# Induced attention and channel mix on one core: the large products as 64-row halves on two row tiles

## The chip, the cores and the metric

The kernel runs on one core of one Trainium2 chip. Five engines work side by side, each through its own queue in order: TensorE (PE in the profile, with its weight loads as PEld), VectorE (DVE), ScalarE (ACT), GpSimd (POOL) and SyncE (SP), whose queue issues nearly all DMAs. The metric is the device time of one execution in microseconds; each number of a run is the median of its executions.

## The reference

Two layers follow each other. The first is attention over 32 inducing points, the second a channel mix with a squared ReLU and a sigmoid gate. Cut to what matters:

```python
# x: (4, 12608, 128); inducing: (32, 128); w_k: (128, 1024); w_v: (1024, 128); w_r: (128, 128)
def mab(q, kv):
    s = scale * (q @ kv.transpose(0, 2, 1))
    a = np.exp(s - s.max(-1, keepdims=True))
    a /= a.sum(-1, keepdims=True) + 1e-09
    return a @ kv
h = mab(I, x)                       # (4, 32, 128)
x = mab(x, h)                       # (4, 12608, 128)
x_prev = np.concatenate([zeros, x[:, :-1, :]], axis=1)      # one token back
xk = mu_k * x + (1.0 - mu_k) * x_prev
xr = mu_r * x + (1.0 - mu_r) * x_prev
k = np.maximum(xk @ w_k, 0.0)
v = k * k @ w_v
r = 1.0 / (1.0 + np.exp(-(xr @ w_r)))
return r * v
```

## The kernel before

**Low rank.** The second attention is never multiplied out. A token's row of x is its 32 weights a times h, so xk @ w_k is a (32 numbers) times h·diag(mu_k)·w_k plus the weights of the token before times h·diag(1−mu_k)·w_k. The kernel makes these small matrices once per batch (tile `W`, in the function `combine`) and keeps for each group of 512 tokens the transposed weights (tile `R`).

**Precision.** Products use fp32r operands. To keep fp32 accuracy each operand is split into a rounded high part and the low rest. In the way up (`up`, lines 780 and 782) the four products high·high, high·low, low·high and low·low of 32 rows each are stacked into the 128 rows of one matmul: `R` holds high, low, high, low, `W` holds high, high, low, low. One such matmul takes the tokens, a second one the tokens shifted by one (a column of `R` ahead of the group, filled by `halo`). In the way down (`down`, line 811) three passes wvh·kh, wvl·kh and wvh·kl run over 128 rows each.

**Units.** A batch has 25 groups (24 of 512 tokens and one of 320). A group has four units, each with two of the eight 128-wide chunks of the 1024 hidden channels; the four batches make 400 units. A unit n issues, in the order that the main loop writes out by hand:

- on PE four matmuls up (128x512 each) into one of two buffers of `ps_a`; two more for the gate (`zgate`) once per group; then the six matmuls down of unit n−4 (`LAG`) into the group's bank `ps_v`;
- on DVE the ReLU (`k_t`, line 792) and, for some units (`high_vector`), the square kh (line 794); otherwise ACT makes kh (797); ACT makes the full square (798);
- on POOL the low part kl = k² − kh (line 800), which the way down reads four units later;
- after a group's last unit, on DVE, the product with the gate (`oT`, 816) and one unit later a transpose (`ot`, 827); every second group SP issues four stores (834).

**Work between the units.** Hand-written tables (`at`, `soon`) put the attention of the batch in hand (`stage_b`) and the first attention of the next batch (`stage_a`, `combine`) behind units. `stage_a` transposes x on DVE (331) and scatters it with four DMAs to `xt` (334), then makes scores (359) and the weighted sum (428) on PE. `stage_b` makes scores (617), softmax, the high and low parts `ah` and `al`, and spreads them with four DMAs per group (671) and one DMA for the halo column (594) into `R`; ten buffers of `R` let this run ahead. Nothing on PE waits for SP other than for a DMA that has landed.

**In the head** a short warm-up (`spin`, lines 895 to 902) runs three 128-row matmuls, four pairs of 64-row matmuls, and three 128-row matmuls again.

Of the kernel before, what the change touches and what calls it, by code (L numbers as in the profile page):

```python
# [8 lines left out]
F32 = mybir.dt.float32  # L9
# [6 lines left out]
EPS = 1e-9  # L16


@with_exitstack
def kernel(  # L20
# [22 lines left out]
    WF = F + C  # L43
# [4 lines left out]
    assert NBLK == 7 and C == P and M * Q == P and F % 1024 == 0 and TAIL % Q == 0  # L48
# [8 lines left out]
    r_pool = ctx.enter_context(tc.tile_pool(name="r_pool", bufs=10))  # L57
# [153 lines left out]
    def stage_a_head(j):  # L211
# [38 lines left out]
        def expo():  # L250
            L.e1t = mp.tile([P, G], F32, name="rT")
# [221 lines left out]
    def combine(b, at=None, t=0):  # L473
# [18 lines left out]
        def weights():  # L492
# [11 lines left out]
            sw = sm.tile([P, P], F32, name="mk", bufs=1)  # L504
            if ahead:
                nc.vector.tensor_scalar(out=sw, in0=stack_f, scalar1=wt, scalar2=rd,
                                        op0=ALU.mult, op1=ALU.mult)
            else:
                nc.vector.tensor_scalar(out=sw, in0=stack_f, scalar1=rd, scalar2=None, op0=ALU.mult)
            L["sw"] = sw  # L510

        def mixed(*parts):
            for nm, mu in parts:
                h4 = L["h4"][nm] = sm.tile([P, P], F32, name="h4" + nm, bufs=1)
                nc.vector.tensor_scalar(out=h4, in0=L["hp"], scalar1=mu, scalar2=None, op0=ALU.mult)

        def hfin():
            ps = pb_tile(None if ahead else "b")
            nc.tensor.matmul(out=ps[:, :P], lhsT=S.acc, rhs=L["sw"], start=True, stop=True)
            h = sm.tile([P, P], F32, name="hT")  # L520
            nc.vector.tensor_copy(out=h, in_=ps[:, :P])
            S.hT = h[:, :M]
            L["hp"] = ps[:, :P]
            L["h4"] = {}
            mixed(("k0", muk), ("k1", omuk))
            mixed(("r0", mur), ("r1", omur))
            S.W = [wp.tile([P, WF], F32R, name=f"W{s}") for s in range(2)]

        def wpart(s, c, tile):

            X = {}
            c0, cw, nm, src = ((F, C, f"r{s}", wr_sb) if c is None else
                               (c * G, G, f"k{s}", wk_sb[:, c * G:(c + 1) * G]))
            dst = S.W[s][:, c0:c0 + cw]

            def prod():
                X["ps"] = tile()[:, :cw]
                nc.tensor.matmul(out=X["ps"], lhsT=L["h4"][nm], rhs=src, start=True, stop=True)

            def high():  # L540
                nc.scalar.copy(out=dst, in_=X["ps"])

            def low():
                nc.vector.tensor_tensor(out=dst[P // 2:], in0=X["ps"][P // 2:, :],
                                        in1=dst.bitcast(F32)[P // 2:], op=ALU.subtract)
            return prod, high, low

        def wpack(parts, cw, tags, t):

            X = {}  # L550
            rows = M * len(parts)

            def prod():
                X["ps"] = pb_tile("a")
                for n, (s, nm, c0, src) in enumerate(parts):
                    nc.tensor.matmul(out=X["ps"][M * n:M * (n + 1), :cw], lhsT=L["h4"][nm][:, :M], rhs=src,
                                     start=True, stop=True)

            def high():
                X["hi"] = st.tile([P, G], F32R, name=tags[0], bufs=tags[2])[:rows, :cw]  # L560
                nc.scalar.copy(out=X["hi"], in_=X["ps"][:rows, :cw])

            def low():
                lo = st.tile([P, G], F32R, name=tags[1], bufs=tags[2])[:rows, :cw]
                hi = X["hi"].bitcast(F32)
                nc.vector.tensor_tensor(out=lo, in0=X["ps"][:rows, :cw], in1=hi, op=ALU.subtract)
                X["hl"] = (hi, lo.bitcast(F32))

            def spread(n):
                s, nm, c0, src = parts[n]  # L570
                for q in range(Q):
                    nc.sync.dma_start(out=S.W[s].bitcast(F32)[M * q:M * (q + 1), c0:c0 + cw],
                                      in_=X["hl"][q // 2][M * n:M * (n + 1)])
            at(t, prod)
            at(t, high)
            at(t + 1, low)
            for n in range(len(parts)):
                at(t + 1 + n, lambda n=n: spread(n))
# [5 lines left out]
        parts = [(s, f"k{s}", c * G, wk_sb[:, c * G:(c + 1) * G]) for c in range(F // G) for s in range(2)]  # L584
        for n in range(0, len(parts), Q):
            wpack(parts[n:n + Q], G, ("ah", "al", 1), t + 11 + 4 * (n // Q))
        wpack([(s, f"r{s}", F, wr_sb) for s in range(2)], C, ("xs", "xs", 3), t + 13)

    def halo(S, g, far=True):

        if g == 0:
            nc.vector.memset(S.R[g].bitcast(F32)[:, 0:1], 0.0)
        elif far:
            nc.sync.dma_start(out=S.R[g].bitcast(F32)[:, 0:1], in_=S.R[g - 1].bitcast(F32)[:, G:G + 1])
        else:
            nc.vector.tensor_copy(out=S.R[g][:, 0:1], in_=S.R[g - 1].bitcast(F32)[:, G:G + 1])


    def stage_b(b, j, at, t):
# [55 lines left out]
        def high():  # L655
            L["ah"] = st.tile([P, G], F32R, name="ah")[:, :w]
            nc.scalar.copy(out=L["ah"], in_=L["aT"])

        def low():
            L["al"] = st.tile([P, G], F32R, name="al")[:, :w]  # L660
            nc.vector.tensor_tensor(out=L["al"], in0=L["aT"], in1=L["ah"].bitcast(F32), op=ALU.subtract)

        def spread(i):
            src = (L["ah"].bitcast(F32), L["al"].bitcast(F32))
            if full or i == 0:
                S.R[j * Q + i] = r_pool.tile([P, G + 1], F32R, name="R")
                halo(S, j * Q + i)
            R = S.R[j * Q + (i if full else 0)].bitcast(F32)
            o, lo = (0, 0) if full else (offs[i], i * w - offs[i])
            for q in range(Q):  # L670
                nc.sync.dma_start(out=R[M * q:M * (q + 1), 1 + o + lo:1 + o + w],
                                  in_=src[q % 2][M * i:M * (i + 1), lo:w])
# [12 lines left out]
        for i in range(Q):  # L685
            at(t + 10 + i, lambda i=i: spread(i))

    def stage_b_head(gs):
# [7 lines left out]
        def scores():  # L696
            ps = L["ps"] = pb_tile("b")
            for k, g in enumerate(gs):
# [5 lines left out]
                S.R[g] = r_pool.tile([P, G + 1], F32R, name="R")  # L704
# [19 lines left out]
        def place(k):  # L724
            g = gs[k]
            X = {}

            def src():
                return L["s2"][:, k * Q:(k + 1) * Q, :].unsqueeze(2).broadcast_to([P, Q, 2, M])

            def high():
                X["a"] = st.tile([P, G], F32R, name=("ah", "al")[g % 2]) \
                    .rearrange("p (k q m) -> p k q m", k=Q, q=Q)
                nc.scalar.copy(out=X["a"][:, :, 0::2, :], in_=src())
# [220 lines left out]
    def start():  # L955
# [9 lines left out]
        def gate_bank(s):  # L965
            if s == 0:
                box["g"] = bank()
# [112 lines left out]
```

## Time and profile before

| | |
|---|---|
| time, median of 3 runs | 1143.82 us (1141.26 to 1147.39) |
| profiled execution | 1144.99 us, its span 1142.9 us, granted clock 0.993 |
| PE busy | 1103.4 us (97%) |
| PEld busy | 837.4 us (73%) |
| DVE busy | 917.7 us (80%) |
| ACT busy | 971.3 us (85%) |
| POOL busy | 948.4 us (83%) |
| chain that ended last, by engine | PE 79%, DVE 8%, ACT 7% |
| DMA moved | 102.32 MB, mean 90 GB/s |

Busy time of PE counts a matmul from its start to the end of its pipeline, so the mean of one (393 ns for 128x512) is longer than the distance to the next start. The share says how seldom PE stands still; the rate is read from the distance between starts. Issuing a DMA holds SP's queue but counts as no engine's busy time.

### The profile page before, as it was taken

To read this page: it belongs to the slowest core of one execution; us is meant where nothing else is said; L and a number is where in the kernel's file an instruction comes from. 1 tells how busy PE (TensorE), PEld (TensorE's weight loads), DVE (VectorE), ACT (ScalarE), POOL (GpSimd) and SP (SyncE) were. 2 spreads that over 40 slices of the span, in tenths; PEclk is the share of its full clock that TensorE was granted. 3 is DMA by queue.
4 is the path that set the end of the run, shared out by engine and by line. 5 is a ranking of instruction groups with operands and counts; after the bars stand their busy time and mean duration, and the time that the engine had idled before them with its cause. 6 is when DMAs were issued, how large, how long until landed. Compare 5 with 4: busy or idle time off the path is not lost.

```text
span 1142.9 us, 17673 instructions
## 1 busy us (share of the span) xinstructions
PE 1103.4 (97%) x5716; PEld 837.4 (73%) x5716; DVE 917.7 (80%) x1294; ACT 971.3 (85%) x1107; POOL 948.4 (83%) x413
## 2 busy tenths in 40 slices
PE   6778999999989999999999999999999999999997
PEld 4456777777777777777877777777778777777886
DVE  5687898987678889897777889898777888887665
ACT  5477889888988888888988988889889988889996
POOL 1157888998887988888889888888888899999996
PEclk9999999999999999999999999999999999999999
DMA  9213444555135455555124455545222233242212
GB/s 275 69 28 91 106 108 111 129 127 108 31 70 119 91 121 124 125 124 124 24 61 87 110 128 120 129 99 124 50 50 61 46 64 59 54 74 56 43 28 34
DMA packets 274988, 102.32 MB, mean 90 GB/s; under 512 B 234288, under 2 KB 249808, under 8 KB 272592
## 3 DMA queue, kind: packets, MB, share of 16 engines
q1 hardware_dynamic: 274560, 101.18, 40.7%
q8 instruction: 45, 0.74, 0.3%
q14 instruction: 47, 0.39, 0.1%
q10 hardware_dynamic: 336, 0.02, 0.0%
HBM read 28.07 MB, written 25.82 MB: 47 GB/s over the span
## 4 chain that ended last, share of the span: by engine, by line
PE 79%; DVE 8%; ACT 7%; issue 3%; SPq 2%; DMA 1%; DVEq 0%; ACTq 0%
PE ps_v L811 40%; PE ps_a L780 15%; PE ps_a L782 13%; DVE k_t L792 3%; PE pb_b L617 2%; PE ps_v L769 2%; PE ps_v L770 2%; PE pb_a L359 2%; ACT kh L797 2%; PE pb_a L428 2%; ACT L772 1%; ACT L634 1%; ACT k_t L798 1%; SPq L93 1%; DVE kh L794 1%
## 5 line engine op out<-in xcount | busy, mean ns | idle before, releaser
L800 POOL TENSOR_TENSOR kl<-k_t,kh 128x1024 fp32r<-128x1024 f32 (+2 forms) x400 | 939.6, 2377 | 154.1 <-ACT k_t L798 136.4
L792 DVE TENSOR_SCALAR k_t<-ps_a 128x1024 f32<-128x1024 f32 (+1 forms) x400 | 480.2, 1201 | 162.1 <-PE ps_a L782 147.0
L798 ACT ACTIVATE k_t<-k_t 128x1024 f32<-128x1024 f32 (+1 forms) x400 | 418.3, 1048 | 46.9 <-DVE kh L794 35.7
L797 ACT ACTIVATE kh<-k_t 128x1024 fp32r<-128x1024 f32 (+1 forms) x352 | 366.0, 1040 | 81.5 <-PE ps_v L811 45.0
L780 PE MATMUL ps_a<-R,W 128*128 128x512 f32 (+1 forms) x800 | 324.5, 406 | 8.9 <-DMA R<-al 4.8
L782 PE MATMUL ps_a<-R,W 128*128 128x512 f32 (+1 forms) x800 | 314.3, 393 | 0.0
L811 PE MATMUL ps_v<-kh,wvh 128*128 128x512 f32 (+1 forms) x800 | 249.8, 393 | 5.3 <-ACT rT L772 4.7
L811 PE MATMUL ps_v<-kh,wvl 128*128 128x512 f32 (+1 forms) x800 | 249.3, 393 | 0.0
L811 PE MATMUL ps_v<-kl,wvh 128*128 128x512 f32 (+1 forms) x800 | 249.1, 392 | 0.1
L780 PEld LDWEIGHTS ps_a<-R,W 128*128 128x128 f32 x800 | 151.4, 189 | 82.9 <-issue 19.9
L811 PEld LDWEIGHTS ps_v<-kh,wvh 128*128 128x128 f32 x800 | 149.4, 189 | 44.0 <-ACT rT L772 10.0
L811 PEld LDWEIGHTS ps_v<-kl,wvh 128*128 128x128 f32 x800 | 150.3, 189 | 34.8 <-POOL kl L800 0.4
L811 PEld LDWEIGHTS ps_v<-kh,wvl 128*128 128x128 f32 x800 | 150.4, 189 | 34.1
L782 PEld LDWEIGHTS ps_a<-R,W 128*128 128x128 f32 x800 | 151.3, 189 | 30.7
L816 DVE TENSOR_TENSOR oT<-ps_v,rT 128x512 f32<-128x512 f32 (+1 forms) x100 | 66.7, 667 | 2.3
L827 DVE STREAM_TRANSPOSE ot<-oT 128x512 f32<-128x512 f32 x96 | 67.2, 700 | 0.0
L794 DVE SCALAR_TENSOR_TENSOR kh<-ps_a,k_t 128x1024 fp32r<-128x1024 f32 x48 | 58.8, 1225 | 5.4 <-DVE k_t L792 0.5
L772 ACT ACTIVATE rT<-ps_v 128x512 f32<-128x512 f32 (+1 forms) x99 | 57.3, 579 | 0.3
L331 DVE STREAM_TRANSPOSE xs<-xb 128x512 f32<-128x512 f32 x72 | 50.0, 694 | 2.5 <-DMA xt<-xs 1.2
L772 ACT ACT_TABLE_LOAD x31 | 39.8, 1283 | 0.5
L769 PE MATMUL ps_v<-R,W 128*128 128x512 f32 (+1 forms) x99 | 39.2, 396 | 0.8 <-DVE oT L816 0.8
L770 PE MATMUL ps_v<-R,W 128*128 128x512 f32 (+1 forms) x99 | 38.9, 393 | 0.0
(196 smaller groups left out, 614.8 us busy)
## 6 DMA issues: line engine op xcount, KB each, us to landing
out_dram<-ot SPq DMA_DIRECT2D x184, 128.0 KB, 3.3
xb<-in_x_dram SPq DMA_DIRECT2D x18, 1024.0 KB, 5.6
xt<-xs SPq DMA_DIRECT2D x288, 64.0 KB, 2.0
R<-ah SPq DMA_DIRECT2D x184, 64.0 KB, 2.0
R<-al SPq DMA_DIRECT2D x184, 64.0 KB, 2.0
kh<-in_x_dram SPq DMA_DIRECT2D x4, 512.0 KB, 7.3
kl<-in_x_dram SPq DMA_DIRECT2D x4, 512.0 KB, 7.5
xb<-in_x_dram SPq DMA_DIRECT2D x8, 256.0 KB, 5.8
```

The lines of the kernel that those rows point to most:

```text
L769: nc.tensor.matmul(out=ps[:, :w], lhsT=S.W[0][:, F:WF], rhs=R[:, 1:w + 1], start=True, stop=False)
L772: nc.scalar.activation(out=self.rT, in_=ps[:, :w], func=AF.Sigmoid)
L780: nc.tensor.matmul(out=ps[:, c, :w], lhsT=S.W[0][:, cs], rhs=R[:, 1:w + 1], start=True, stop=False)
L782: nc.tensor.matmul(out=ps[:, c, :w], lhsT=S.W[1][:, cs], rhs=R[:, 0:w], start=False, stop=True)
L792: nc.vector.tensor_scalar(out=k, in0=self.ps[:, :, :w], scalar1=0.0, scalar2=None, op0=ALU.max)
L794: nc.vector.scalar_tensor_tensor(out=kh, in0=self.ps[:, :, :w], scalar=0.0, in1=k, op0=ALU.max, op1=ALU.mult)
L797: nc.scalar.activation(out=kh, in_=k, func=AF.Square)
L798: nc.scalar.activation(out=k, in_=k, func=AF.Square)
L800: return lambda eng, a, z: eng.tensor_tensor(out=kl[:, :, a:z], in0=k[:, :, a:z], in1=kh.bitcast(F32)[:, :, a:z], op=ALU.subtract)
L811: nc.tensor.matmul(out=self.v, lhsT=wt[:, fc, :], rhs=kk[:, c, :], start=(fc == 0 and n == 0), stop=(fc == FC - 1 and n == 2))
L816: nc.vector.tensor_tensor(out=self.oT, in0=self.v, in1=self.rT, op=ALU.mult)
L827: nc.vector.transpose(out=ot[:, o:o + w], in_=self.oT)
```

## The change

**Way up.** The 32-row parts are stacked anew. Rows 0 to 63 of `W` belong to the even chunk of a unit, rows 64 to 127 to the odd one; in each half 32 rows act on the tokens and 32 on the tokens shifted by one. There are two `W` tiles, high and low, and `R` has a high and a low plane ([128, 2, 512]). Each chunk needs three passes of 64 rows (high·high, low·high, high·low) on its own row tile of PE: six 64-row matmuls per unit instead of four 128-row ones. The low·low product is dropped. The small matrices come out of PE in their final place, so the DMAs that spread `W` go.

**Way down.** Each of the six 128-row matmuls is split into two 64-row ones. The lower half of unit n−4 runs on row tile 0 while the upper half of unit n−5 runs on row tile 1. Groups go in pairs with their units alternating, so that the two row tiles write different `ps_v` banks at a time. The gate of both groups of a pair is computed at the pair's unit 6, one group on each row tile.

**A relay.** Since the next unit's row tile 0 goes on in the bank that row tile 1 has just written, or the other way round, each unit's first way-down matmul waits for the last matmul of the unit before. The wait goes through SP: a no-op on SP waits for that matmul, and PE waits for the no-op. The no-op is written right after the unit's matmuls, ahead of the stores and the events of that unit.

**Spreading.** `R` has four buffers, so a group is spread when the pair before the last has been read (`free`), with four DMAs of twice the size and two halo DMAs. `kh` has 6 buffers and `kl` 5 instead of 4 each. The event tables start 4 units earlier (batches after the first) or 2 (the first).

```diff
-    r_pool = ctx.enter_context(tc.tile_pool(name="r_pool", bufs=10))
+    r_pool = ctx.enter_context(tc.tile_pool(name="r_pool", bufs=NR))        # NR = 4
...
+    def new_r(S, g):
+        R = S.R[g] = r_pool.tile([P, 2, G], F32R, name="R")
+        rf = R.bitcast(F32)
+        for r in (M, 3 * M):
+            if g == 0:
+                nc.vector.memset(rf[r:r + M, :, 0:1], 0.0)
+            else:
+                nc.sync.dma_start(out=rf[r:r + M, :, 0:1], in_=S.R[g - 1].bitcast(F32)[:M, :, G - 1:G])
+        return rf
+    def fill(rf, src, o, n, width, first=0):
+        for q in range(first, Q):
+            s = q % 2
+            m = min(n, width - o - s)
+            nc.sync.dma_start(out=rf[M * q:M * (q + 1), :, o + s:o + s + m], in_=src[:, :, :m])
...
-        for i in range(Q):
-            at(t + 10 + i, lambda i=i: spread(i))
+        for i in range(Q if full else 1):
+            f = b * NG + j * Q + i
+            free = 2 * NU * (f // 2 - 1) - 1 + 2 * (f % 2)
+            at(max(t + 10, free), lambda i=i: spread(i))
...
+        def passes(self, ps, r, cs):
+            rows = slice(HP * r, HP * (r + 1))
+            S, R, w = self.S, self.S.R[self.g], self.w
+            for n, (a, k) in enumerate(((0, 0), (1, 0), (0, 1))):
+                yield lambda n=n, a=a, k=k: nc.tensor.matmul(
+                    out=ps, lhsT=S.W[a][rows, cs], rhs=R[rows, k, :w], start=(n == 0), stop=(n == 2))
         def up(self, u):
-            for c in range(UC):
-                cs = slice((u * UC + c) * P, (u * UC + c + 1) * P)
-                nc.tensor.matmul(out=ps[:, c, :w], lhsT=S.W[0][:, cs], rhs=R[:, 1:w + 1], ...)
-                nc.tensor.matmul(out=ps[:, c, :w], lhsT=S.W[1][:, cs], rhs=R[:, 0:w], ...)
+            cs = slice(u * P, (u + 1) * P)
+            return [list(self.passes(self.ps[:, r, :self.w], r, cs)) for r in range(2)]
...
-        def down(self, u):
+        def down(self, u, r):
+            rows = slice(HP * r, HP * (r + 1))
             for n, (wt, kk) in enumerate(((wvh, kh), (wvl, kh), (wvh, kl))):
                 for c in range(UC):
                     fc = u * UC + c
-                    nc.tensor.matmul(out=self.v, lhsT=wt[:, fc, :], rhs=kk[:, c, :], ...)
+                    th.append(lambda ...: nc.tensor.matmul(
+                        out=self.v, lhsT=wt[rows, fc, :], rhs=kk[rows, c, :], ...))
...
+    units = [(flat[p + r], u) for p in range(0, len(flat), 2) for u in range(NU) for r in range(2)]
...
+        for n in range(len(units) + LAG + 1):
+            (grp, u), (old, ou), (last, lu) = unit(n), unit(n - LAG), unit(n - LAG - 1)
+            upward = grp.up(u) if grp is not None else [[], []]
+            low = old.down(ou, 0) if old is not None else []
+            high = last.down(lu, 1) if last is not None else []
+            if grp is not None and n % (2 * NU) == ZSTEP:                   # ZSTEP = 6
+                z, sigmoid = zgate([units[n][0], units[n + 1][0]])
+                upward = [upward[r] + z[r] for r in range(2)]
+            ends = last is not None and lu == NU - 1
+            lead = 2 if ends and grp is not None else len(upward[1])
+            order = [upward[0] + low, upward[1][:lead] + high + upward[1][lead:]]
+            for k in range(max(map(len, order))):
+                for r, th in enumerate(order):
+                    for f in th[k:k + 1]:
+                        ins = f().ins
+                        if k >= lead and relay is not None:
+                            tc.add_manual_dep(ins, relay, SYNC)
+                            relay = None
+            if low or high:
+                nop = nc.sync.nop().ins
+                tc.add_manual_dep(nop, ins.name, SYNC)
+                relay = nop.name
+            if ends:
+                last.gate()
+            if grp is not None:
...
+                sub = grp.square(u, n in high_vector)
...
+            if ends:
+                last.store()
             run(events.pop(n, []))
```

**The order on PE.** Two units of the middle of the run before; the name in brackets is what a row waits for (Activation is ACT, Pool is POOL).

```order
L780 MATMUL ps_a<-R,W_3318 128x512 [waits DVE_49]
L782 MATMUL ps_a<-R,W_3319 128x512
L780 MATMUL ps_a<-R,W_3318 128x512
L782 MATMUL ps_a<-R,W_3319 128x512
L811 MATMUL ps_v<-kh,wvh 128x512 [waits Activation_49]
L811 MATMUL ps_v<-kh,wvh 128x512
L811 MATMUL ps_v<-kh,wvl 128x512 x2
L811 MATMUL ps_v<-kl,wvh 128x512 [waits Pool_49]
L811 MATMUL ps_v<-kl,wvh 128x512
```

The same place after; the sizes are those of the output, and the matmuls alternate between the row tiles.

```order
L747 MATMUL ps_a<-R,W_7611 128x512 [waits DVE_49]
L747 MATMUL ps_a<-R,W_7611 128x512
L747 MATMUL ps_a<-R,W_7612 128x512 x2
L747 MATMUL ps_a<-R,W_7611 128x512 x2
L784 MATMUL ps_v<-kh,wvh 128x512 [waits SP_sequencer_49,Activation_49]
L784 MATMUL ps_v<-kh,wvh 128x512 x3
L784 MATMUL ps_v<-kh,wvl 128x512 x4
L784 MATMUL ps_v<-kl,wvh 128x512 [waits Pool_49]
L784 MATMUL ps_v<-kl,wvh 128x512 x3
```

Ten 128-row matmuls have become eighteen 64-row ones, and the first of the way down now waits for SP's queue as well as for ACT.

**The order on SP**, before, around a store in batch 1 (event waits and no-ops are not listed in such an order).

```order
L334 DMA xt<-xs 32x512 [waits DMAHW2_49]
L204 DMA xb<-in_x_dram 128x2048 [waits DMAHW3_49,PE_49]
L834 DMA out_dram<-ot 32x32x32 [waits DMAHW4_49,DVE_49]
L834 DMA out_dram<-ot 32x32x32 [waits DMAHW5_49]
L834 DMA out_dram<-ot 32x32x32 [waits DMAHW6_49]
L834 DMA out_dram<-ot 32x32x32 [waits DMAHW7_49]
L594 DMA R<-R 128x1 [waits DMAHW0_49]
```

After, in the same batch: a scatter of x (`xt`), a spread of one group (`R`, lines 567 and 575) and a store.

```order
L337 DMA xt<-xs 32x512 [waits DMAHW2_49,DVE_49]
L337 DMA xt<-xs 32x512 [waits DMAHW3_49]
L337 DMA xt<-xs 32x512 [waits DMAHW4_49]
L337 DMA xt<-xs 32x512 [waits DMAHW5_49]
L567 DMA R<-R 32x2x1 [waits PE_49,DMAHW6_49]
L567 DMA R<-R 32x2x1 [waits DMAHW7_49]
L575 DMA R<-hl 32x1024 [waits DMAHW0_49]
L575 DMA R<-hl 32x2x511 [waits DMAHW1_49]
L575 DMA R<-hl 32x1024 [waits DMAHW2_49]
L575 DMA R<-hl 32x2x511 [waits DMAHW3_49]
L809 DMA out_dram<-ot 32x32x32 [waits PE_49,DMAHW4_49,DVE_49]
```

A spread has six DMAs instead of five, and between the units' batches of DMAs on this queue now stand the 400 no-ops that PE waits for.

**The order on DVE** at the end of a group before: the gate's product, then two ReLUs (792) and a square ahead of the transpose that the stores wait for.

```order
L816 TENSOR_TENSOR oT<-ps_v,rT 128x320 [waits PE_49]
L792 TENSOR_SCALAR k_t<-ps_a 128x1024 [waits PE_49,Pool_49]
L794 SCALAR_TENSOR_TENSOR kh<-ps_a,k_t 128x1024 [waits DVE_49,PE_49]
L792 TENSOR_SCALAR k_t<-ps_a 128x1024 [waits PE_49,Pool_49]
L827 STREAM_TRANSPOSE aT<-oT 128x320
```

After, at the end of both groups of a pair (762 is the ReLU, 791 the gate's product, 802 the transpose).

```order
L791 TENSOR_TENSOR oT<-ps_v,rT 128x512 [waits PE_49]
L762 TENSOR_SCALAR k_t<-ps_a 128x1024 [waits PE_49,Pool_49]
L802 STREAM_TRANSPOSE ot<-oT 128x512 [waits DVE_49]
L791 TENSOR_TENSOR oT<-ps_v,rT 128x512 [waits DVE_49,PE_49]
L762 TENSOR_SCALAR k_t<-ps_a 128x1024 [waits PE_49,Pool_49]
L802 STREAM_TRANSPOSE ot<-oT 128x512 [waits DMAHW6_49,DMAHW5_49,DMAHW7_49,DMAHW0_49,DVE_49]
```

The gate's product now waits for the matmuls of its own unit and stands ahead of that unit's ReLU, and the transpose follows in the same unit.

More of the change, by code (lines that the diff above doesn't have):

```diff
@@ L529, in wpart @@
-        def wpart(s, c, tile):
+            nc.tensor.matmul(out=ps[:, :M], lhsT=S.acc, rhs=L["sw"], start=True, stop=True)
+            S.hT = sm.tile([P, M], F32, name="hT")
+            nc.vector.tensor_copy(out=S.hT, in_=ps[:, :M])
+            h4 = L["h4"] = sm.tile([P, Q, M], F32, name="h4", bufs=1)
+            for n, mu in enumerate((muk, omuk, mur, omur)):
+                nc.vector.tensor_scalar(out=h4[:, n, :], in0=ps[:, :M], scalar1=mu, scalar2=None, op0=ALU.mult)
+            S.W = [wp.tile([P, WC], F32R, name=f"W{s}") for s in range(2)]
@@ L531, in wpart @@
+        def wpart(gate, tile):
             X = {}
-            c0, cw, nm, src = ((F, C, f"r{s}", wr_sb) if c is None else
-                               (c * G, G, f"k{s}", wk_sb[:, c * G:(c + 1) * G]))
-            dst = S.W[s][:, c0:c0 + cw]
+            c0, cw = (F // 2, C) if gate else (0, F // 2)
             def prod():
                 X["ps"] = tile()[:, :cw]
-                nc.tensor.matmul(out=X["ps"], lhsT=L["h4"][nm], rhs=src, start=True, stop=True)
+                chunks = wk_sb.rearrange("p (c e d) -> p e c d", e=2, d=P)
+                for n in range(Q):
+                    o = X["ps"][M * n:M * (n + 1), :]
+                    if not gate:
+                        o = o.rearrange("m (c d) -> m c d", d=P)
+                    nc.tensor.matmul(out=o, lhsT=L["h4"][:, 2 * gate + n % 2, :],
+                                     rhs=wr_sb if gate else chunks[:, n // 2], start=True, stop=True)
@@ L546, in wpart @@
             return prod, high, low
[L548 to L578, printed above, removed]
@@ L583, in combine @@
         at(t + 10, hfin)
[L584 to L596, printed above, removed]
+        for gate in range(2):
+            prod, high, low = wpart(gate, lambda: pb_tile("a"))
+            at(t + 11 + 2 * gate, prod)
+            at(t + 11 + 2 * gate, high)
+            at(t + 12 + 2 * gate, low)
+    def new_r(S, g):
[12 more added lines that the diff above has]
+            nc.sync.dma_start(out=rf[M * q:M * (q + 1), :, o + s:o + s + m], in_=src[:, :, :m])
     def stage_b(b, j, at, t):
@@ L748, in stage_b_head, with high, low @@
-        return scores, diff, expo, norm, [place(k) for k in range(len(gs))]
+        def high():
+            a = L["a"] = st.tile([P, 2, G], F32R, name="hl", bufs=2) \
+                .rearrange("p s t -> p (s t)")[:, :2 * n * M].rearrange("p (k s m) -> p k s m", s=2, m=M)
+            nc.scalar.copy(out=a[:, :, 0, :], in_=L["s2"])
+        def low():
+            nc.vector.tensor_tensor(out=L["a"][:, :, 1, :], in0=L["s2"], in1=L["a"].bitcast(F32)[:, :, 0, :],
+                                    op=ALU.subtract)
@@ new lines, in put @@
+        def put(k, whole):
+            g = gs[k]
+            ps = pa.tile([P, 2, G], F32, name="ps_a")
+            for c in range(Q):
+                for s in range(2):
+                    nc.tensor.transpose(out=ps[:M, s, c * P:(c + 1) * P], identity=ident,
+                                        in_=L["a"].bitcast(F32)[:, k * Q + c, s, :])
+            rf = new_r(S, g)
+            R = S.R[g]
+            nc.scalar.copy(out=R[:M], in_=ps[:M])
+            if whole:
+                for q in range(1, Q):
+                    s = q % 2
+                    eng = nc.vector.tensor_copy if s else nc.scalar.copy
+                    eng(out=R[M * q:M * (q + 1), :, s:], in_=ps[:M, :, :G - s])
+            else:
+                fill(rf, rf[:M], 0, G, G, 1)
@@ L751 @@
+        return scores, diff, expo, norm, high, low, put
     NG = (NBLK - 1) * Q + 1
@@ L847, in halves @@
     def halves():
[L849 removed]
+        for name, n in (("kh", 6), ("kl", 5)):
             for _ in range(4):
[L851 removed]
+                yield mp.tile([P, UC, G], F32, name=name, bufs=n)
     pairs = halves()
```

212 lines of the change are left out of this document (71 added, 141 removed).

## The prediction

> I forecast a loss: 1355 us against 1143.82 us. PE's own work shrinks by a tenth, but the new relay puts SP's queue, with its slow DMA issues, into PE's path.
>
> **What bounds the kernel now.** First the page's busy times, its chain and its costliest groups: who is full, and what the end hangs on.
>
> ```profile
> PE 1103.4 (97%) x5716; PEld 837.4 (73%) x5716; DVE 917.7 (80%) x1294; ACT 971.3 (85%) x1107; POOL 948.4 (83%) x413
> PE 79%; DVE 8%; ACT 7%; issue 3%; SPq 2%; DMA 1%; DVEq 0%; ACTq 0%
> L800 POOL TENSOR_TENSOR kl<-k_t,kh 128x1024 fp32r<-128x1024 f32 (+2 forms) x400 | 939.6, 2377 | 154.1 <-ACT k_t L798 136.4
> L792 DVE TENSOR_SCALAR k_t<-ps_a 128x1024 f32<-128x1024 f32 (+1 forms) x400 | 480.2, 1201 | 162.1 <-PE ps_a L782 147.0
> L794 DVE SCALAR_TENSOR_TENSOR kh<-ps_a,k_t 128x1024 fp32r<-128x1024 f32 x48 | 58.8, 1225 | 5.4 <-DVE k_t L792 0.5
> L816 DVE TENSOR_TENSOR oT<-ps_v,rT 128x512 f32<-128x512 f32 (+1 forms) x100 | 66.7, 667 | 2.3
> L827 DVE STREAM_TRANSPOSE ot<-oT 128x512 f32<-128x512 f32 x96 | 67.2, 700 | 0.0
> L331 DVE STREAM_TRANSPOSE xs<-xb 128x512 f32<-128x512 f32 x72 | 50.0, 694 | 2.5 <-DMA xt<-xs 1.2
> ```
>
> PE carries the end: 79% of the chain, and DVE's ReLU waits 147 us in total for PE's `ps_a`. POOL comes next: its 400 differences take 939.6 us. Then the timeline of PE, in the middle of the run, for the real rate; the columns are start and length.
>
> ```profile
> 503.27 0.40 PE L780 MATMUL ps_a<-R,W 128*128 128x512 f32 x1
> 505.14 0.63 PE L811 MATMUL ps_v<-kl,wvh 128*128 128x512 f32 x2
> 505.60 0.39 PE L780 MATMUL ps_a<-R,W 128*128 128x512 f32 x1
> ```
>
> The unit's ten matmuls take 2.33 us from one unit's start to the next (503.27 to 505.60), 0.233 us each, though each one lasts 0.4 us. Behind some units stands other PE work, for example the scores:
>
> ```profile
> 499.85 1.07 PE L359 MATMUL pb_a<-xt,indT 128*32 128x512 f32 x8
> 500.85 0.50 PE L780 MATMUL ps_a<-R,W 128*128 128x512 f32 x1
> ```
>
> Such a piece costs 1.0 us (499.85 to 500.85), before and after alike.
>
> **Do halves run side by side?** The head's warm-up shows it. These rows are the timeline cut at three narrow stretches.
>
> ```profile
> 44.79 0.95 PE L895 MATMUL ps_a<-wvh 128*128 128x512 f32 x3
> 46.24 0.40 PE L899 MATMUL ps_a<-wvh 64*128 64x512 f32 x2
> 46.47 0.41 PE L899 MATMUL ps_a<-wvh 64*128 64x512 f32 x2
> 46.80 0.96 PE L902 MATMUL ps_a<-wvh 128*128 128x512 f32 x3
> ```
>
> Two 64-row matmuls on two row tiles, each with its own weight load, take 0.23 us together (46.24 to 46.47), the price of one 128-row matmul. So a pair of halves counts as one.
>
> **The change, part by part.** *PE's large products.* Before, 10 per unit and 2 per group of four units for the gate: 10.5 × 0.233 = 2.45 us. After, 3 pairs up, 6 down, and 3 per eight units for the two gates: 9.375 × 0.233 = 2.18 us. That is 0.26 us in 400 units, 105 us off the engine that sets the end. Alone it would give 1145 − 105 = 1040 us (the profiled execution took 1145 us with a span of 1142.9; the median is 1 us lower).
>
> *What would come next without stalls* is POOL, which must fit 939.6 us from its first difference to the end:
>
> ```profile
> L800 POOL TENSOR_TENSOR kl<-k_t,kh x400: 882/2413/2542, 64.6 to 1134.5; 128x1024 fp32r<-128x1024 f32 x128, 128x640 fp32r<-128x640 f32 x5, 128x320 fp32r<-128x320 f32 x1
> ```
>
> 64.6 + 939.6 + the 8.4 us after its last start (1134.5 to 1142.9) is 1013 us, below 1040: no bound, but close. The DMAs that spread `W` fall away at no gain on PE, since they were issued beside it. The head loses a few small products and gains four copies; the first difference would start where it does now (64.6), within 5 us either way. Work from the tables moves 2 to 4 units earlier, which costs nothing as long as the relay is what PE waits for.
>
> *The relay.* SP works off its queue in order. The no-op of unit n stands behind all DMAs that were written after unit n−1, and unit n+1's way down stands behind that no-op. How long SP holds its queue for a DMA is in its timeline:
>
> ```profile
> 854.08 1.22 SPq L572 DMA_DIRECT2D W<-ah  x2
> 855.35 1.22 SPq L572 DMA_DIRECT2D W<-al  x2
> 856.67 2.43 SPq L572 DMA_DIRECT2D W<-xs  x4
> 859.15 1.22 SPq L572 DMA_DIRECT2D W<-ah  x2
> ...
> 698.88 2.42 SPq L334 DMA_DIRECT2D xt<-xs  x4
> 701.41 3.03 SPq L834 DMA_DIRECT2D out_dram<-ot  x4
> 704.54 0.70 SPq L204 DMA_DIRECT2D xb<-in_x_dram  x1
> ...
> 510.44 0.51 SPq L594 DMA_DIRECT2D R<-R  x1
> 510.99 0.60 SPq L671 DMA_DIRECT2D R<-ah  x1
> ```
>
> Eight DMAs in a row take 5.07 us (854.08 to 859.15), 0.63 us each; four take 2.42 us, and one with nothing ahead of it 0.51. I take 0.62 us each, 2.75 for four stores (between 2.42 and 3.03). The 1 MB load's 0.70 us against 0.60 for 64 KB says that the doubled size of a spread's DMAs hardly matters: the bounds for one are 0.51 and 0.70.
>
> The price of a signal from PE to another engine, from one row of each:
>
> ```profile
> 707.00 0.40 PE L782 MATMUL ps_a<-R,W 128*128 128x512 f32 x1
> 707.51 1.22 DVE L792 TENSOR_SCALAR k_t<-ps_a 128x1024 f32<-128x1024 f32 x1 [0.40 <-PE ps_a L782]
> ```
>
> The matmul ends at 707.40 and DVE starts at 707.51: 0.11 us. I take it for both legs, 0.22 us.
>
> *What is hidden.* From the end of unit n's matmuls PE has unit n+1 (9 pairs, 2.10 us) and unit n+2's way up (3 pairs, 0.70) before it needs the no-op of n+1; the last matmul's end lies 0.17 us (0.40 − 0.23) behind the next slot, and the legs take 0.22. That leaves 2.4 us for the batch of DMAs of unit n, plus 1.0 us for each piece of other PE work there and 0.7 for the gates. A no-op with an empty batch ahead of it has 0.3 us to spare (0.70 − 0.17 − 0.22) and costs nothing; if that cover is too short by 0.2 us, 207 empty batches cost 41 us (upper bound). A longer batch stops PE for the rest, and PE can't make it up, being only one way up ahead.
>
> *Waits for data inside a batch.* Stores wait for DVE: after the unit's matmuls come the gate's product, that unit's ReLU and the transpose, 0.67 + 1.20 + 0.70, less the 0.23 that the group's last matmul stands ahead: 2.4 us with a signal. Before, the same wait cost PE nothing although SP sat in it:
>
> ```profile
> SPq L834 <- DVE ot L827: 134.7, 29, 16.8
> ```
>
> The scatter `xt` waits for its transpose (0.69 us), which follows the ReLU; the ReLU ends about with its unit's matmuls (they come 6 pairs, 1.4 us, after its input), so 0.6 us. Spreads wait for nothing: their data is made a unit or more earlier. The order lets each DMA wait for the eighth one ahead of it to land, and a group's first matmul for its spread:
>
> ```profile
> out_dram<-ot SPq DMA_DIRECT2D x184, 128.0 KB, 3.3
> R<-ah SPq DMA_DIRECT2D x184, 64.0 KB, 2.0
> ```
>
> Landing takes 2.0 to 3.3 us, eight issues take 5.0, and a spread is issued seven units (15 us) or more before its group in most cases: both hidden.
>
> *Who waits behind it.* Behind PE's waiting way down stand the rest of that unit, the tables' PE work and the next way up; then DVE waits for `ps_a` and for the bank that the gate's product reads, and POOL for a `kl` buffer, which is free once the upper half five units back is through. They only wait longer; nothing of theirs ends later than PE. On DVE the gate's product, waiting for PE, now holds up its unit's ReLU, which the way down needs four units later: hidden.
>
> *The sum over batches.* The order on SP gives the batches between the no-ops. Each line: wait + issue, less 2.4, less the other PE work that the order on PE shows there on average.
>
> - 58 spreads of one group (6 DMAs): 3.7 − 2.4 − 0.5 = 0.8, 46 us.
> - 24 spreads with a scatter (10): 6.2 − 2.4 − 0.4 = 3.4, 82 us.
> - 43 stores (4, three with a load): 2.4 + 2.75 − 2.4 − 0.75 = 2.0, 86 us.
> - 7 stores with a scatter (8): 2.4 + 5.2 − 2.4 − 0.7 = 4.5, 31 us.
> - 4 spreads of the 320-token groups (18): 11.2 − 2.4 − 0.3 = 8.5, 34 us.
> - 6 rarer ones (9 to 16 DMAs): together 37 us.
> - 33 scatters alone: 0.6 + 2.5 − 2.4 − 1.1, below 0. Loads, single pieces and 207 empty ones: 0.
>
> Stalls: 316 us. 1145 − 105 + 316 = 1356; I say **1355**. POOL, DVE and ACT use the stalls to catch up, so their own work adds nothing.
>
> *Bounds.* Without waits for data and with 0.56 us per DMA (0.51 and 0.05 to the next) the lines give 29, 67, 0, 11, 30 and some 25 us, 162 in all: 1202. With 41 us for empty batches, 25 for stores at 3.03 us and more, and 13 for one store in four behind which DVE also makes kh (1.2 us), it is 1435.
>
> [...]
>
> **The rivals.** *SP's batches don't reach PE (faster).* If an issue held the queue for no more than 0.24 us, ten DMAs would fit into the 2.4 us of cover and only the 105 us would be left: 1040, up to 1055 with POOL so close. For it: before, DMAs never stopped PE for long. Against it: the rows above, in which each DMA starts only after the one ahead has left the queue. The point that decides is 0.24 against 0.62. Chance 0.09.
>
> *A milder loss, 1150 to 1225.* Stores don't wait, because DVE reaches the transpose earlier, and issues take 0.51. For it: DVE has slack once PE stalls. Against: the gate's product can't start before the unit's last way down. Chance 0.06.
>
> *Halves take turns.* If two halves cost 0.46 instead of 0.23, the way up and down would take 18.75 × 0.233 = 4.37 us a unit, 1.92 more: 1145 + 768 = 1913. The warm-up speaks against it, though its halves read one tile and never changed their banks. [...] With all else above 1435: chance 0.05.
>
> **How the numbers follow.** The forecast, 1225 to 1435, has 0.80; 0.09 lie at 1040 to 1055, 0.06 between 1150 and 1225, 0.05 above. Its range starts above the lower bound because both short values would have to hold at once. A measurement of this kernel tells about 0.5% from no change; only an odd balance of 105 us and the stalls would end there: 0.01. Faster 0.09, slower 0.90.
>
> **What would show it.** PE's distance between pairs: 0.23. Idle time ahead of the way down, line 784, released by SP, some 300 us in total; a batch of ten DMAs on SP over 6 us, and the next way down right behind its no-op; units with empty batches near 2.2 us, so an uneven PE. POOL's and PE's busy shares fall below 80%. In the last batch, without scatters, a pair of groups takes 17.5 us of PE and some 4 us of stalls. I am wrong if PE waits for SP by less than 100 us, if pairs take longer than 0.25 us, or if stores turn out to start right behind their no-op.

## The result, and the profile after

| | before | after |
|---|---|---|
| median | 1145.22 us | 1564.53 us (1561.97 to 1566.13) |
| ratio | | 1.3665, 95% interval 1.3619 to 1.3710 |
| span of the profiled execution | 1142.9 us | 1560.0 us |
| mean granted TensorE clock | 0.993 | 0.901 |

Slower, as forecast, but by 419 us where 211 were forecast; 1564 is outside 1225 to 1435. Rows of the page after: busy times, granted clock, chain, and groups.

```profile
PE 1155.5 (74%) x9048; PEld 844.1 (54%) x9048; DVE 915.4 (59%) x1291; ACT 979.1 (63%) x1060; POOL 944.9 (61%) x413
PEclk9797899999888797897989899999998989998889
PE 39%; SPq 25%; DVE 17%; issue 8%; ACT 6%; DMA 3%; POOL 1%; DVEq 0%; ACTq 0%; POOLq 0%
L762 DVE TENSOR_SCALAR k_t<-ps_a 128x1024 f32<-128x1024 f32 (+1 forms) x400 | 479.1, 1199 | 354.8 <-PE ps_a L747 350.6
L747 PE MATMUL ps_a<-R,W 64*128 64x512 f32 (+1 forms) x2700 | 471.7, 423 | 143.9 <-SPq L1013 90.9
L784 PE MATMUL ps_v<-kh,wvh 64*128 64x512 f32 (+1 forms) x1600 | 323.1, 438 | 225.3 <-SPq L1013 198.4
L791 DVE TENSOR_TENSOR oT<-ps_v,rT 128x512 f32<-128x512 f32 (+1 forms) x100 | 67.8, 678 | 182.7 <-PE ps_v L784 179.7
```

SP's queue, 2% of the chain before, holds a quarter of it: L1013 is the relay's no-op. The vector engines do the same work as before in a longer time. The surprise is in the first row: PE has a tenth less to do and is busy 52 us longer. The windows of one stall say why; the columns are the stretch, busy time (and instructions) of PE, PEld, DVE, ACT and POOL, the granted clock, DMA share and GB/s.

```profile
690.00:699.20 9.20, 9.20 (x73) 7.55 (x71) 4.74 (x7) 4.87 (x5) 4.48 (x2) 0.81 0.19 43
699.20:704.30 5.10, 0.91 (x8) 0.47 (x5) 3.21 (x4) 4.98 (x9) 4.17 (x3) 0.94 0.60 134
704.30:710.70 6.40, 6.34 (x30) 4.61 (x32) 1.49 (x2) 0.70 (x1) 3.23 (x2) 0.51 0.18 39
710.70:714.00 3.30, 3.30 (x54) 2.44 (x52) 0.92 (x5) 2.12 (x2) 0.75 (x1) 1.00 0.54 124
```

And the timelines of SP and of PE around it:

```profile
698.84 2.52 SPq L575 DMA_DIRECT2D R<-hl  x4
701.79 2.45 SPq L337 DMA_DIRECT2D xt<-xs  x4
```

```profile
704.36 1.22 PE L784 MATMUL ps_v<-kh,wvh 64*128 64x512 f32 x4 [4.25 <-SPq L1013]
705.38 1.05 PE L784 MATMUL ps_v<-kh,wvl 64*128 64x512 f32 x4
706.23 1.05 PE L784 MATMUL ps_v<-kl,wvh 64*128 64x512 f32 x4
```

The last scatter leaves SP's queue at 704.24; the no-op follows at 704.29 and PE's way down at 704.36, after 4.25 us of idle PE. Then two pairs take 0.85 us (705.38 to 706.23), 0.43 each instead of 0.23, for 6.4 us at a clock of 0.51. So the stall costs its length and about 3 us more.

Over the whole trace (PE's matmuls merged into stretches, and the records of the clock): before, 37 stretches with 30 us of idle time between them, and PE busy for 13.7 us at half clock. After, 227 stretches, 395 us idle, of which 313 end right behind the relay's no-op, and 229 us busy at half clock. Half clock began within an idle stretch or up to 1 us behind it for 6 of 68 stretches of 1 to 2 us, 12 of 25 of 2 to 3 us, 8 of 10 of 3 to 4 us, and 24 of 27 that were longer. It came in 56 spells, each 3.41, 6.83 or 10.24 us long (one, at the end, 5.14). So the longer an idle stretch, the more often half clock followed.

The sum that fits: PE's busy time 1103 − 105 = 998, plus (229 − 14) / 2 = 108 lost to half clock (a pair takes 0.43 us there instead of 0.23, so about half is lost), plus 49 for 190 more stretches at some 0.26 us each: the last matmul of a stretch is seen to its end, 0.16 us, and the first step behind the stop is 0.10 us longer than the others, both in the median at full clock. Together 1155. With 365 us more idle time than before: 1143 − 105 + 365 + 157 = 1560.

### The profile page after: what moved, and what is told of

It is laid out like the page before. It is cut to its first block, busy times and chain, and to the rows that moved or that the text cites. A ratio compares the mean times of both kernels' runs of the same rounds, so it can differ in the third digit from the quotient of the medians.

```text
span 1560.0 us, 24951 instructions
## 1 busy us (share of the span) xinstructions
PE 1155.5 (74%) x9048; PEld 844.1 (54%) x9048; DVE 915.4 (59%) x1291; ACT 979.1 (63%) x1060; POOL 944.9 (61%) x413
## 4 chain that ended last, share of the span: by engine, by line
PE 39%; SPq 25%; DVE 17%; issue 8%; ACT 6%; DMA 3%; POOL 1%; DVEq 0%; ACTq 0%; POOLq 0%
PE ps_v L784 23%; SPq L575 12%; PE ps_a L747 11%; DVE k_t L762 8%; SPq L337 6%; SPq L567 4%; SPq L809 3%; DVE ot L802 2%; ACT kh L767 2%; PE pb_b L595 2%; ACT k_t L768 1%; DVE oT L791 1%; DMA R<-hl 1%; PE pb_a L362 1%; DVE xs L334 1%
## 5 line engine op out<-in xcount | busy, mean ns | idle before, releaser
L747 PE MATMUL ps_a<-R,W 64*128 64x512 f32 (+1 forms) x2700 | 471.7, 423 | 143.9 <-SPq L1013 90.9
L784 PE MATMUL ps_v<-kh,wvh 64*128 64x512 f32 (+1 forms) x1600 | 323.1, 438 | 225.3 <-SPq L1013 198.4
L747 PEld LDWEIGHTS ps_a<-R,W 64*128 64x128 f32 x2700 | 303.2, 200 | 274.1 <-SPq L1013 108.2
L784 PEld LDWEIGHTS ps_v<-kh,wvh 64*128 64x128 f32 x1600 | 176.2, 202 | 297.8 <-SPq L1013 126.4
L784 PE MATMUL ps_v<-kl,wvh 64*128 64x512 f32 (+1 forms) x1600 | 308.6, 415 | 0.0
L784 PE MATMUL ps_v<-kh,wvl 64*128 64x512 f32 (+1 forms) x1600 | 302.7, 414 | 0.0
L784 PEld LDWEIGHTS ps_v<-kl,wvh 64*128 64x128 f32 x1600 | 199.9, 202 | 26.9
L784 PEld LDWEIGHTS ps_v<-kh,wvl 64*128 64x128 f32 x1600 | 196.5, 201 | 27.5
L791 DVE TENSOR_TENSOR oT<-ps_v,rT 128x512 f32<-128x512 f32 (+1 forms) x100 | 67.8, 678 | 182.7 <-PE ps_v L784 179.7
L981 ACT ACTIVATE rT<-ps_a 128x1024 f32<-128x1024 f32 x46 | 47.2, 1026 | 34.6 <-PE ps_a L747 34.3
L764 DVE SCALAR_TENSOR_TENSOR kh<-ps_a,k_t 128x1024 fp32r<-128x1024 f32 (+1 forms) x48 | 58.0, 1208 | 1.7
L635 ACT CAST hl<-pb_b 128x512 fp32r<-128x512 f32 (+1 forms) x27 | 14.0, 520 | 34.6 <-DMA R<-hl 34.6
```

The costliest lines, as they stand in the source:

```text
L747: yield lambda n=n, a=a, k=k: nc.tensor.matmul(out=ps, lhsT=S.W[a][rows, cs], rhs=R[rows, k, :w], start=(n == 0), stop=(n == 2))
L784: th.append(lambda n=n, c=c, fc=fc, wt=wt, kk=kk: nc.tensor.matmul(out=self.v, lhsT=wt[rows, fc, :], rhs=kk[rows, c, :], start=(r == 0 and ...
L791: nc.vector.tensor_tensor(out=self.oT, in0=self.v, in1=self.rT, op=ALU.mult)
L981: nc.scalar.activation(out=rT, in_=ps, func=AF.Sigmoid)
```

## The experiments

Theory A: the loss is the relay behind SP's DMA issues, by the stalls' length and the half clock that they bring. Theory B: the halves themselves hold PE. Theory C: whatever else holds PE in the shorter units (DVE, ACT, POOL) takes back what the relay gives. Some of the expectations give the letters a narrower sense of their own, C above all; what they say there holds for their run.

**SP's batches split.** At most 4 DMAs behind one no-op; stores and scatters a unit later, when their data is ready.

```diff
-                nc.sync.dma_start(out=S.xt[j, i][M * c:M * (c + 1), :], in_=xs[M * i:M * (i + 1)])
+                put_off(now[0] + 1, now[0] + 3, lambda i=i: nc.sync.dma_start(...))
...             # spreads and stores alike
             run(events.pop(n, []))
+            issue(n, 4 if n < LAST[0] - 1 else 99)
```

> Only the DMAs' places on SP change: spreads, scatters and stores of a unit are handed out over the next units, at most four per unit where their due times allow it, and stores and scatters one unit after the DVE work that they wait for; all matmuls, no-ops and the number of DMAs stay. Theory A (PE waits for SP's batches through the relay, and those waits cost once more by PE's halved clock and restarts): four DMAs take 2.5 us, about the cover of 2.4 us, so nearly all of the 312 us of waits and of the half-clock time go: 1065 us (1045 to 1110), below the kernel before. Theory B (the 64-row halves or the three passes themselves are slow in the full kernel): above 1300 us. Theory C (SP is too full as a whole, so splitting only moves the waits): 1150 to 1300 us.

1273.69 us, ratio 1.1126 (1.1095 to 1.1156). 291 us come from nothing but other places in SP's queue.

```profile
PE 1078.9 (85%) x9048; PEld 786.6 (62%) x9048; DVE 915.4 (72%) x1291; ACT 972.7 (76%) x1060; POOL 946.1 (74%) x413
PE ps_a L771 <- DVE k_t L786: 33.9, 34, 6.4
PE ps_a L771 <- SPq L1039: 29.9, 44, 4.4
PE ps_v L808 <- SPq L1039: 25.5, 44, 2.9
```

Relay stalls fall to 60 us, PE's busy time at half clock to 47. A's direction is right, its 1065 us is not. The time lies in C's range, but the waits did not only move: of the 183 us that PE is still idle, 57 are put down to SP, the rest mostly to DVE (76) and ACT (30). There are 231 units with four DMAs, 138 of them right behind another such unit, and then SP needs 4 × 0.62 us and, as an estimate, about 0.45 for the no-op's round each time (the 2.88 us below leave 0.40 for it). The 2.4 us of cover is one unit's slack once, no allowance that each unit gets anew; units with four DMAs took 2.88 us in the median (2.6 to 4.0 for most), empty ones in the changed kernel 2.06.

**Only the stores later**, by the same `put_off`, nothing else.

> The changed kernel with its stores alone issued one unit later, after the DVE transpose has run. Theory A: the stores' waits for data inside a batch are in PE's path; the 50 batches with a store held PE for 44 + 28 us in the trace; most of the 44 go and some clock loss with them: 1500 to 1530 us. Theory B (SP's wait for DVE there is hidden, since DVE and PE are late anyway): 1555 to 1570 us. My prediction's own size of this term, 86 us, would give 1450 to 1480 us.

1524.02 us in a single execution, in A's range: 40 us less, not the 86 that the prediction gave the stores.

**Filler work in the stalls.** 730 pairs of 64-row matmuls, overwritten by the unit's own, at the start of the 41 units that waited longest.

```diff
+            for k in range(FILL.get(n, 0) if grp is not None else 0):
+                for r in range(2):
+                    nc.tensor.matmul(out=grp.ps[:, r, :grp.w], lhsT=grp.S.W[0][HP * r:HP * (r + 1), :P], ...)
```

> The changed kernel with 730 pairs of matmuls whose results are overwritten at once (the first pass up, repeated), 11 to 35 pairs ahead of the way up of the 41 units whose way down waits longest for SP. They fill the waits and add no wait. Theory A (PE's clock falls to half after idle stretches, and that costs about 107 us of the 229 us that PE works at half clock): 1440 to 1490 us, the half-clock time falls from 310 us to under 120 us. Theory B (half clock lies beside the waits and costs nothing): 1560 us or up to 40 us more.

1539.37 us in a single execution, between A's range and B's.

```profile
PE 1268.4 (83%) x10508; PEld 958.6 (62%) x10508; DVE 918.1 (60%) x1291; ACT 980.5 (64%) x1060; POOL 947.1 (62%) x413
```

The filler takes 168 us (730 pairs at 0.23); idle time falls only by 135, to 259, so it overshot by 33 us. But the run is 23 us shorter although idle time and filler together grew to 427 us: PE's own work took 1268.4 − 168 = 1100 us instead of 1155.5, and its busy time at half clock fell from 229 to 117. Half of that fall is 56 us, and 55 are gone from PE's own work. So the clock is the second part of the loss, as far as one execution shows it.

**The relay alone**, in the kernel before: whole matmuls, and each unit's first way-down matmul behind a no-op of the unit before.

```diff
+                    if relay:
+                        tc.add_manual_dep(ins, relay.pop(), SYNC)
+            nop = nc.sync.nop().ins
+            tc.add_manual_dep(nop, ins.name, SYNC)
+            relay.append(nop.name)
```

> The kernel before with nothing but the relay added: each unit's first way-down matmul waits for a no-op on SP that waits for the last matmul of the unit before; 128-row products, ten R buffers and old DMAs stay. Theory A (the relay alone makes the loss): cover 2.9 us; 38 batches of nine DMAs 88 us, 37 stores 75, nine batches of thirteen 45, others some 30, with clock and restarts 60 to 90 more: 1460 us (1380 to 1510). Theory B (the loss comes with the halves, the four R buffers or the doubled spreads): 1145 to 1200 us.

1506.73 us in a single execution, in A's range: 361 us lost without the change's halves; in its trace 277 us idle, 213 busy at half clock.

```profile
PE ps_v L812 <- SPq L816: 241.4, 124, 6.0
```

**The relay on POOL.** POOL has one kind of work; each subtraction goes behind the next unit's no-op.

```diff
-                nop = nc.sync.nop().ins
+                nop = nc.gpsimd.nop().ins
...
+            run(behind)                       # the subtraction of the unit before
...
-                sub(nc.gpsimd, 0, part)
+                    behind.append(lambda sub=sub, part=part: sub(nc.gpsimd, 0, part))
```

> The changed kernel with the relay's no-op on POOL's queue instead of SP's, and each unit's subtraction (L770, 2353 ns) given to POOL behind that no-op, so one unit later. SP keeps every DMA and PE waits for none of them. Theory A (the loss is the relay standing behind DMA issues, and the half clock that its stalls bring): POOL's cycle becomes 2.35 + about 0.1 us a unit, so 400 units give 980 us, head and tail 60, and the stalls of other origin seen in the changed kernel (about 80 us, partly in POOL's shadow) 20 to 80: 1060 to 1130 us, half-clock time below 60 us. Theory B (the halves themselves, their restarts or the two row tiles, hold PE, whatever carries the relay): above 1300 us. Theory C (a relay through another engine's queue only moves the wait there): 1150 to 1300 us, with waits released by POOL of over 100 us.

1237.43 us, ratio 1.0818 (1.0792 to 1.0844): 327 us back, but longer than A allows. B, above 1300 us, is ruled out. The time is in C's range, but not by what C named there, a wait of over 100 us for POOL:

```profile
PE ps_a L747 <- DVE k_t L762: 43.2, 40, 5.3
PE ps_v L784 <- ACT k_t L768: 17.5, 15, 1.4
PE ps_a L747 <- ACT rT L981: 15.5, 9, 4.5
PE ps_v L784 <- POOLq L1014: 3.1, 6, 0.9
```

POOL's no-op holds PE for 5 us in all, 3 of them at the way down. What is left over the kernel before: 130 us more idle time, now mostly for DVE and ACT (79 and 52 us of all 160), 25 for half clock, some 35 for restarts. It takes back all of the 105 us. So the halves bring about what was forecast, and the waits for DVE and ACT, theory C in the sense given at the head of this section, eat it.

**The same, the subtractions in their old place.**

> The same with the subtractions left where they are: the no-op of a unit stands behind the subtraction of the unit before it, which waits for that unit's ReLU and squares. Theory A: a loop over three units of upward products, ReLU 1.2, square 1.05, second square 1.05, subtraction 2.35, no-op and downward products of 1.5 us, together about 7.8 us or 2.6 us a unit: 1110 to 1200 us, slower than with the subtraction moved. Theory C: the wait for POOL is paid each unit in full (1.5 to 2.5 us): above 1500 us. Theory B: above 1300 us.

1293.26 us, ratio 1.1293 (1.1269 to 1.1318): above A's 1200, far from C's full price, and 7 us below B's range. Of PE's idle time 84 us end behind POOL's no-op. The order inside the queue that carries the relay is worth 56 us.

**The relay on POOL in the kernel before.** As in the run with the relay alone, but with the no-op on POOL and each unit's subtraction moved behind the unit's own no-op.

> The kernel before with nothing but a relay between its units, as in the earlier run, with the no-op on POOL ahead of the subtraction instead of on SP. Theory A: the 361 us that the relay on SP cost go, but for the round trip: 1145 to 1200 us. Theory B says nothing of it. Theory C: 1250 to 1500 us, part of the loss stays whatever queue carries the relay.

1184.83 us, ratio 1.0346 (1.0324 to 1.0369), as A said. POOL's queue costs 40 us where SP's cost 361.

```profile
PE ps_v L812 <- POOLq L816: 40.4, 48, 1.7
```

**Fewer issues on SP.** The split run with at most 3 DMAs a unit, and the one-column halos as copies on DVE.

```diff
-                nc.sync.dma_start(out=rf[r:r + M, :, 0:1], in_=S.R[g - 1].bitcast(F32)[:M, :, G - 1:G])
+                    events.setdefault(now[0] + HALO, []).append(lambda r=r, old=old:
+                        nc.vector.tensor_copy(out=R[r:r + M, :, 0:1], in_=S.R[g - 1][:M, :, G - 1:G]))
```

> The relay stays on SP; the 192 one-column DMAs of the spreads become copies on DVE (about 0.1 to 0.2 us each, three units later), and at most 3 DMAs go behind one no-op where the earlier split run allowed 4. Theory A: a batch of 3 takes 3 x 0.62 + 0.45 = 2.3 us, about one unit, so of the earlier 231 batches of four only 78 stay, at about 0.55 us each: 1274 - 153 x 0.55 - 30 to 45 of clock = 1150, 1130 to 1190 us. A rival (what is left of the split run's loss is not SP's any more but DVE's and ACT's waits): 1220 to 1280 us.

1365.14 us, ratio 1.1921 (1.1896 to 1.1946): neither. SP did its part (waits put down to it 21 us instead of 57), but the 182 copies took 890 ns each on average, not 0.1 to 0.2 us.

```profile
L589 DVE CAST R<-R 32x2 fp32r<-32x2 f32 x182 | 162.0, 890 | 3.3
PE ps_v L815 <- DVE oT L822: 70.5, 35, 4.6
PE ps_a L778 <- DVE k_t L793: 65.5, 39, 6.2
```

**Upward halves alone.** The way down whole again, so that no relay is needed.

```diff
-            low = old.down(ou, 0) if old is not None else []
-            high = last.down(lu, 1) if last is not None else []
+            low = old.down(ou) if old is not None else []          # six 128-row matmuls
...             # no relay, no no-op
```

> One part of the change alone: the upward products as 64-row halves in three passes, pairs of groups and just-in-time spreads as in the changed kernel, but the downward products whole (six 128-row matmuls a unit), so that no relay is needed at all. PE has the same 9.375 slots a unit. Theory A (the loss was the relay, its half clock, and short waits for DVE and ACT, which have less room in a shorter unit): 1143 - 105 = 1038 us, and between nothing and what the run with the relay on POOL showed beyond the kernel before (125 us of waits, 31 of half clock): 1040 to 1195, 1100 as the middle. Theory B (a row of 64-row pairs costs something each time PE changes between them and whole matmuls, 0.1 to 0.25 us at 800 changes): 1180 to 1350 us with PE busy over 1080.

1232.18 us, ratio 1.0751 (1.0728 to 1.0773): in B's range. PE is idle for 67 us only, but busy for 1152.9.

```profile
PE 1152.9 (94%) x6648; PEld 707.7 (58%) x6648; DVE 915.0 (74%) x1291; ACT 974.6 (79%) x1060; POOL 946.2 (77%) x413
```

That is what B named, a price for each change between pairs and whole matmuls; the next run shows its size.

**And a third `hl` buffer** (`kh` 5 instead of 6).

> The same with three buffers instead of two for the split attention tiles (hl, from which the spreads are sent) and five instead of six for kh, which whole downward products allow. ACT waited 34.6 us in the changed kernel for a spread out of an hl buffer to land, up to 13.5 us at a time. Theory A: 10 to 40 us faster than the run before it. If ACT's waits do not reach PE: the same within 5 us.

1220.31 us, ratio 1.0652 (1.0619 to 1.0686): 12 us faster; ACT no longer waits for an `hl` buffer at all. A unit of it on PE's timeline:

```profile
700.30 0.97 PE L747 MATMUL ps_a<-R,W 64*128 64x512 f32 x6
701.20 0.73 PE L782 MATMUL ps_v<-kh,wvh 128*128 128x512 f32 x2
701.76 0.62 PE L782 MATMUL ps_v<-kh,wvl 128*128 128x512 f32 x2
702.22 0.62 PE L782 MATMUL ps_v<-kl,wvh 128*128 128x512 f32 x2
702.78 0.96 PE L747 MATMUL ps_a<-R,W 64*128 64x512 f32 x6
```

Two whole matmuls between others of their kind take 0.46 us (701.76 to 702.22); the two behind the change of shape take 0.56, and so do the two ahead of the next. The unit takes 2.48 us where nine slots of 0.231 would be 2.08: 0.2 us for each change, 160 us in 400 units. The trace gives the price of a change; what PE does in that time it does not show.

**Half the changes of shape.** Two units' upward products stand together ahead of their ways down.

```diff
+            if n < 8 or n % 2 == 0:
+                for k in range(n, min(n + (2 if n >= 8 else 1), len(units))):
+                    for pair in zip(*units[k][0].up(units[k][1])):
+                        run(pair)
```

> As the run before it (upward halves, whole downward products, three hl buffers), but from unit 8 on the upward products of two units stand together ahead of their downward products, and a gate's product follows the second of them. In the two runs before, the last matmul ahead of a change between 64-row pairs and whole matmuls took 0.327 us to the next start instead of 0.231, and the first behind it 0.340: 0.2 us a change, 0.4 us a unit, 160 us in all. Theory A (that is the price, and it is paid per change): half the changes go, 196 x 0.41 = 80 us, 1220 - 80 = 1140 us, 1125 to 1175 with what DVE and ACT make PE wait in the longer bursts of upward work; the kernel before runs 1145. Theory B (the slow pitch belongs to a unit or to waiting weights and not to a change of shape): 1205 to 1230.

1216.14 us, ratio 1.0627 (1.0610 to 1.0643). PE's busy time falls by 44 us to 1104.2, 71 without what the clock and 66 more restarts add (10 and 17), of the 80 expected: the price is paid per change. But idle time rises from 60 to 100 us: with two units of upward work in a row PE waits for DVE's ReLU 69 times.

```profile
PE ps_a L748 <- DVE k_t L764: 44.8, 69, 1.5
PE ps_a L748 <- DVE kh L766: 18.5, 14, 2.8
```

**DVE's 48 squares to ACT** in that kernel (`high_vector` empty).

> As the run before it, but the 48 squares that DVE computes from PSUM (L766, 1.21 us each, 58 us) go to ACT like the other 352 (1.04 us each, 50 us more on ACT). Theory A (what still holds PE in the shorter units is DVE's ReLU coming late, 65 us of waits): the 18.5 us of waits for these squares go and the waits for the ReLU fall by a third, with some clock: 1216 - 18 - 15 - 10 = 1173, 1160 to 1195 us. Rival (DVE and ACT are equally tight, and ACT becomes late in its place): 1205 to 1240 us, with new waits for ACT of over 30 us.

1188.75 us, ratio 1.0366 (1.0335 to 1.0397), in A's range, and ACT did not become late. The waits for the squares are gone and half clock costs 10 us less; the waits for the ReLU did not fall (47.2 us, 71 times), against A. Of all versions with halves this is the fastest; none beat the kernel before.

## Why the prediction was right or wrong

- *PE's gain of 105 us*: right. Pairs started 0.231 us apart in the median at full clock, in the changed kernel and in the run with the relay on POOL. PE's busy time less half clock and restarts is 998 us in the one and 1007 in the other, where 1103 − 105 = 998 was forecast.
- *The relay's stalls, 316 us*: right in kind, and in the sum partly by luck, 313 measured. In its lines: spreads 58 us for 46, spreads with a scatter 86 for 82, stores with a scatter 28 for 31, the 320-token spreads 37 for 34, the rarer ones 36 for 37; but stores 44 for 86, and scatters alone 19 for 0. What the stores were given too much, the scatters and spreads had too little. The stores' first issue did wait, 2.13 us behind the no-op for 2.4 forecast; a stall of 1.06 us each instead of 2.0 was left. A batch of ten DMAs took 6.72 us from no-op to no-op on average and held PE for 3.6 where 3.4 was forecast, so the cover was about as forecast; that it is slack for one batch and not for each showed in the split run.
- *The step that failed*: "A longer batch stops PE for the rest". A stall was priced by its length. But most stalls over 3 us (32 of 37) and half of those of 2 to 3 us are followed by a spell at half clock, 3.41 to 10.24 us long, and each stop costs a restart, together 108 + 49 = 157 us on PE's busy time, of which the prediction had none. It read the clock nowhere, though the page has a row for it. These 157 us and the 52 of the next point are the 209 us that the forecast fell short.
- *"Hidden" and "their own work adds nothing"*: wrong by 52 us, the idle time beyond the relay's 313 and the 30 of before. PE waits for the ReLU and for DVE's square, where it hardly did before. The likely way, which no run tests alone: the gate's product, which waits for the relayed way down (179.7 us of DVE's idle time), stands ahead of its unit's ReLU on DVE, so a stall is passed on to the next unit's `ps_a`. And "Spreads wait for nothing" overlooked that the spread just in time holds an `hl` buffer, for which ACT waited 34.6 us; a third buffer, in the kernel with whole ways down, gave 12 us.

```profile
PE ps_a L747 <- DVE k_t L762: 26.3, 22, 7.6
PE ps_a L747 <- DVE kh L764: 6.2, 6, 1.5
L635 ACT CAST hl<-pb_b 128x512 fp32r<-128x512 f32 (+1 forms) x27 | 14.0, 520 | 34.6 <-DMA R<-hl 34.6
```

- *1040 without stalls*: also too low, and no rival said so. POOL was named as the next bound; the run with the relay on POOL shows DVE and ACT instead, though they are busy for 74% and 79% of it only: 130 us more idle time of PE. It would be their bursts and not their totals; the runs show the waits, not what a burst costs.
- *The rivals*: batches did reach PE (313 us of stalls behind the no-op); the milder loss did not come: the stores' first issue did wait (2.13 us), and the sum with the trace's 0.62 us an issue fits (in the changed kernel 0.63 from one start to the next). Halves did not take turns (0.231 us a pair). By these sums a gain of this kernel's halves would need both a relay in another queue and DVE and ACT on time; no run reached it.

## What to carry to other kernels

A relay through an engine's queue costs what stands ahead of it there: give it to the queue with the shortest and most even work, and let its own order put the relay first; 361 us on SP became 40 on POOL, with the subtractions moved behind the no-op and nothing else changed. Price a stall of PE by its length and by the clock that follows (here 24 of 27 stops over 4 us were followed by half clock, 6 of 68 of 1 to 2 us), and a shorter unit by whether the other engines' bursts still fit into it. Where 64-row pairs and whole matmuls of 512 columns alternate, add the 0.2 us measured here for each change.

## What the runs showed of the hardware

A small DVE copy from SBUF to SBUF waited for POOL. In the run with halos as copies, 100 of 182 took under 0.3 us, 0.16 in the median, and only one of them lies inside a subtraction of POOL, from 2 ns after its start. The other 82 took 0.30 to 2.37 us; each started inside a subtraction and ended 0.02 to 0.03 us after a subtraction did. DVE's and POOL's timelines at one place:

```profile
210.33 4.54 DVE L589 CAST R<-R 32x2 fp32r<-32x2 f32 x2
```

```profile
210.07 4.78 POOL L801 TENSOR_TENSOR kl<-k_t,kh 128x1024 fp32r<-128x1024 f32 x2
```

Two copies of two columns last as long as two subtractions. DVE's ReLU, which reads PSUM, takes 1.22 us in the median inside a subtraction of this run and 1.22 outside. What the trace shows is a full wait for the running subtraction; what ties the copy to it, it does not tell.

The half-clock spells of the kernel before last 3.41 us (4 of them), those of the changed one 3.41 (29), 6.83 (17) or 10.24 us (9), but for the last one of each trace (4.76 and 5.14 us). And the change between 64-row and whole matmuls, 0.2 us, was expected by no step of the prediction, though the warm-up that it read shows it: the last pair starts at 46.47 and the whole matmul behind it at 46.80, 0.33 us instead of 0.23.
